# Moving the second weight's widening and part of the second inverse stage behind the first group

## The chip, the cores and the metric

The kernel runs on one core of one Trainium2 chip. The time is device microseconds of that core, the median of several executions. The engines are PE (matmuls), DVE (elementwise, two-input arithmetic), ACT (copies and activations), POOL (elementwise from on-chip memory) and SP, whose queue issues every DMA of this kernel. Each engine works its own instructions off in order.

## The reference

```python
# x: (8, 3136, 256); filt_r, filt_i: (1569, 256); w_ch1: (256, 1024); w_ch2: (1024, 256)
X = np.fft.rfft(x, axis=1)
y = np.fft.irfft(X * (filt_r + 1j * filt_i), n=3136, axis=1)
u = y + np.real(np.fft.fft(np.fft.fft(y, axis=1), axis=2))
un = (u - mean(u)) / np.sqrt(var(u) + 1e-6)        # over the last axis
out = u + np.maximum(un @ w_ch1, 0) @ w_ch2
```

## The kernel before, in words

Eight batches go through two pipelines that share the engines.

**The transform pipeline**, once a batch. `forward1` loads seven pieces of x (L379), takes their largest value (L267) to set a scale (`pow2` on DVE, PE and DVE again, then `spread`), splits x into a high and a low half (L394, L395), multiplies (L400) and stores the result in DRAM as d1 (L404). `forward2` loads d1 back as `at` (L425), multiplies with the second stage's table (L449, L450), applies the filters, and runs the first inverse stage (`inverse1`, L514 to L516), whose result goes to DRAM as d2 (L520). `inverse2` is the second inverse stage. It has 14 pieces c = 0 to 13: a load `b` for each pair of pieces (L554), four or eight matmuls (L577, called y_c below), a scaling copy on ACT into `ys` (L584), and, after each pair, four to six stores into DRAM as dy (L560). A pair covers 224 of the batch's 1568 slots.

**The group pipeline**. The slots of all batches are cut into groups of 256. `fetch(g)` reads a group's dy back (L633), `prepare(g)` adds the channel mix (L646 on PE, L656 on DVE), normalizes (L713 to L736) and makes two half-precision halves u16 (L739, L741). For group 0 the transposed `ut` comes from PE transposes (`flip`, L274 and L275); later groups use a DMA transpose (L746). Then eight steps f: `first_product` makes h (six matmuls L770, then L779 on ACT and L780 on DVE), and `second_product`, two steps later, adds twelve matmuls L799 into acc. The result goes through L808 to the output (L811). A group needs both weights: w1s in the first product, w2s in the second.

**The weights** come as 64-bit words. `widen_weights(i)` makes 32-bit numbers of piece i (0 to 3 are w1, 4 to 7 are w2) with four DVE instructions (L819, L820, L821, L825) and three on ACT (L824 between L820 and L825, and the two rows of L829, a sum of squares). `bound_weights` turns the sums into a scale (L865 to L868, with one PE transpose), `split_weights` spreads it with one PE matmul (called pb_w2 for w2; L263, L264), scales on ACT (L882), makes the high half on ACT (L883) and the low half on POOL (L884).

**What sets the order.** The program is written in an order of its own; a scheduler then orders each engine's queue, and `after(...)` puts the instructions of a block behind a marked instruction on its engine. `weigh(n)` emits the weight steps whose number in WIDEN_AT, BOUND_AT and SPLIT_AT is at most n; `give(n)` emits pieces of the second inverse stage, and `bring(slot)` as many as a slot needs. Before group 0 is fetched, pieces 0 to 3 of batch 0 are emitted. While `prepare(0)` runs, each of its steps is followed by another piece and by weight steps up to that number. The first steps of group 0 start at the lines after `bring(511)`.

Of the kernel before, what the change touches and what calls it, by code (L numbers as in the profile page):

```python
# [45 lines left out]
LOAD_AT = (19, 20, 21, 22, 50, 50, 54, 54)  # L46
LOAD_AFTER = (("d1", 10), ("d1", 11), ("d1", 12), ("d1", 13), ("bt", 3), ("bt", 3), ("bt", 4), ("bt", 4))
LOAD_IN = ("ut", "ut", "ys", "ys", "big", "big", "big", "big")
WIDEN_AT = (58, 59, 60, 61, 62, 63, 64, 65)
BOUND_AT = (62, 66)  # L50
SPLIT_AT = (63, 115)
FILTERS_AT = (2, 0, 1, 4, 6, 3, 8, 5)
FILTERS_ON_ACT = (0, 3, 4, 6)

# [140 lines left out]
def _program(ctx, tc, nc, a, NB):  # L195
# [6 lines left out]
    ps_f = ctx.enter_context(tc.tile_pool(name="ps_f", bufs=4, space=PSUM))  # L202
# [3 lines left out]
    marks = {}  # L206

    def bank(name):
        return ps_f.tile([128, 512], F32, tag="psf", name=name)
# [4 lines left out]
    def after(*keys):  # L214

        order = ExitStack()
        for k in keys:
            if k in marks:
                order.enter_context(tc.issue_after(marks[k]))
        return order  # L220
# [9 lines left out]
    ident16 = cp.tile([128, 128], F16, name="ident16")  # L230
# [38 lines left out]
    def flip(dst, src, pool, tag, name):  # L269

        m, n, q = src.shape
        pt = pool.tile([128, 8, 128], F16, tag=tag, name=name)
        for i in range(n):
            nc.tensor.transpose(pt[:q, i, :m], src[:, i], ident16[:m, :m])  # L274
        return nc.scalar.copy(dst, pt[:q, :n, :m])  # L275


# [360 lines left out]
    def channels(p, lhs, start, stop):  # L638

        work = [  # L640
# [3 lines left out]
        ]  # L644
        for i, (c0, n, hs, hm, w0) in enumerate(work):
            nc.tensor.matmul(  # L646
                p[:, c0 : c0 + n],
                lhs(int(i > 2), hs),
                mix[:, hm, w0 : w0 + n],
                start=start and i == 0,  # L650
                stop=stop and i == 7,
            )
# [5 lines left out]
    def add(o, pm, al):  # L658

        n = o.shape[0]  # L660
        oh = o.rearrange("p k (h c) -> p (k h) c", h=2)
        even = pm[:, 1:128].unsqueeze(1).to_broadcast([n, 4, 127])
        odd = pm[:, 129:].unsqueeze(1).to_broadcast([n, 2, 127])
        ends = pm[:, 0:129:128].unsqueeze(1).to_broadcast([n, 2, 2])
        scaled_add(oh[..., 1:], even, al[:, 0:1], oh[..., 1:])
        for hs, sign in ((slice(0, 4, 3), 0), (slice(1, 3), 1)):
            scaled_add(oh[:, hs, 1:], odd, al[:, sign : sign + 1], oh[:, hs, 1:])
        scaled_add(o[..., 0:129:128], ends, al[:, 0:1], o[..., 0:129:128])
# [9 lines left out]
    def prepare(g):  # L678
        tiles = groups[g]
        y = ys_of.pop(g)  # L680
        pm = bank(f"mix_{g}").rearrange("p (t c) -> p t c", t=2)
        fix = []
        for t, (g0, g1) in enumerate(tiles):
            n = g1 - g0
            r0 = g0 % RING
            channels(pm[:n, t], lambda e, h: eo[:, e, h, r0 : r0 + n], t == 0, t == len(tiles) - 1)
            for b in range(NB):
                if g0 <= b * NS < g1:
                    p0 = b * NS - g0
                    pn = bank(f"nyq_{g}_{t}")[p0 : p0 + 1, :256]  # L690
                    channels(pn, lambda e, h: esps[b][:, h, e : e + 1], True, True)
                    fix.append((t, slice(p0, p0 + 1), pn, alphas[b]))
            mixed[0] = g1
            yield
        for t, s, _, _ in fix:
            keep = mp.tile([128, 2, 256], F32, tag="un", name=f"keep_{g}", bufs=2)[:, 0]
            nc.scalar.copy(keep[s], y[s, t, 1])
        for t, (g0, g1) in enumerate(tiles):
            ps = slice(0, g1 - g0)
            with after(("u16", 0)) if g == 1 else after("h"):  # L700
                add(y[ps, t], pm[ps, t], alpha_of(g0, g1, f"al_{g}_{t}")[ps])
        for t, s, pn, al in fix:
            add_nyquist(y[s, t, 1], pn, al[s], keep[s])
        yield
        ut = mp.tile([128, 2, 8, 128], F16, tag="ut", name=f"ut_{g}", bufs=2)
        mv = tp.tile([128, 4, 2], F32, tag="mv", name=f"mv_{g}")
        st = tp.tile([128, 4, 6], F32, tag="st", name=f"st_{g}")
        n = tiles[0][1] - tiles[0][0]
        nt = 2 * len(tiles)
        for t, (g0, g1) in enumerate(tiles):  # L710
            m = g1 - g0
            for k in range(2):
                nc.vector.bn_stats(st[:m, 2 * t + k], y[:m, t, k])  # L713
                nc.vector.bn_aggr(mv[:m, 2 * t + k], st[:m, 2 * t + k])
        sb = tp.tile([128, 4, 4], F32, tag="sb", name=f"sb_{g}")
        parts = [(n, slice(0, nt))]
        if len(tiles) == 2 and tiles[1][1] - tiles[1][0] != n:
            parts = [(n, slice(0, 2)), (tiles[1][1] - tiles[1][0], slice(2, 4))]
        for m, ks in parts:
            nc.scalar.activation(sb[:m, ks, 0], mv[:m, ks, 1], AF.Sqrt, bias=eps[:m])  # L720
        yield
        for m, ks in parts:
            mu, v = mv[:m, ks, 0], mv[:m, ks, 1]
            r, q, c, s = (sb[:m, ks, i] for i in range(4))
            nc.vector.reciprocal(r, r)
            nc.vector.scalar_tensor_tensor(q, r, -8.0, r, op0=ALU.mult, op1=ALU.mult)
            nc.vector.scalar_tensor_tensor(c, v, EPS, q, op0=ALU.add, op1=ALU.mult)
            nc.vector.scalar_tensor_tensor(s, c, 24.0, r, op0=ALU.add, op1=ALU.mult)
            marks["un", g] = nc.vector.scalar_tensor_tensor(q, mu, -1.0, s, op0=ALU.mult, op1=ALU.mult).ins  # L729
        yield  # L730
        for t, (g0, g1) in enumerate(tiles):
            m = g1 - g0
            un = mp.tile([128, 2, 256], F32, tag="un", name=f"un_{g}_{t}", bufs=2)
            for k in range(2):
                i = 2 * t + k
                nc.scalar.activation(un[:m, k], y[:m, t, k], AF.Identity, bias=sb[:m, i, 1:2], scale=sb[:m, i, 3:4])  # L736
            u16 = mp.tile([128, 2, 2, 2, 128], F16, tag="u16", name=f"u16_{g}_{t}", bufs=2)
            unv = un[:m].rearrange("p k (d q) -> p k d q", q=128)
            nc.scalar.copy(u16[:m, :, :, 0], unv)  # L739
            low = nc.vector if g < 2 else nc.gpsimd  # L740
            marks["u16", g] = low.tensor_tensor(u16[:m, :, :, 1], unv, u16[:m, :, :, 0], op=ALU.subtract).ins  # L741
            if g == 0:
                ub = u16[:m].rearrange("p k d l q -> p (k d l) q")
                flip(ut[:, t, :, :m], ub, ps_f, "psf", f"utt_{t}")
            else:
                marks["sp"] = marks["ut", g] = nc.sync.dma_start_transpose(  # L746
                    ut[:, t, :, :m], u16[:m].rearrange("p k d l q -> p (k d l q)")
                ).ins
            yield
        ready[g] = (y, ut)  # L750
# [146 lines left out]
    done, come = [0], [0]  # L897

    def advance(n):

        while done[0] < min(n, NB * STEPS):
            b, s = divmod(done[0], STEPS)
            if s == 0 and come[0] < BACK * (b - 1) + 1:
                return
            if s in folds and b * NS + folds[s] - RING > mixed[0]:
                return
            next(forth)
            done[0] += 1

    def give(n):  # L910

        while come[0] < min(n, NB * BACK) and done[0] >= STEPS * (come[0] // BACK + 1) - 1:
            next(home)
            come[0] += 1
# [11 lines left out]
    def bring(slot):  # L926
        advance(STEPS * (slot // NS + 1) - 1)
        give(need(slot))
        assert come[0] >= need(slot)

    todo = [(n, load_weights, i) for i, n in enumerate(LOAD_AT)]
    todo += [(n, widen_weights, i) for i, n in enumerate(WIDEN_AT)]
    todo += [(n, f, w) for f, at in ((bound_weights, BOUND_AT), (split_weights, SPLIT_AT)) for n, w in zip(at, ("w1", "w2"))]
    todo.sort(key=lambda t: t[0])
# [29 lines left out]
    fetch(0)  # L964
    for i, _ in enumerate(prepare(0)):
        weigh(STEPS + come[0] + i)
        give(come[0] + 1)
    with after(("un", 0)):
        weigh(1000)
    bring(511)  # L970
    fetch(1)
    work = prepare(1)
    for _ in range(AHEAD):
        next(work, None)
    per = NS // 32
    for q in range(8 * ng + LAG):
        g, f = divmod(q, 8)
# [70 lines left out]
```

## Time and profile before

| | |
|---|---|
| median of three runs | 1537.51 us (1533.45 to 1542.68) |
| the profiled execution's own time | 1535.77 us |
| its span | 1534.0 us |
| granted clock of PE, mean | 0.955 |
| PE busy | 1398.7 us (91% of the span) |
| DVE, ACT, POOL busy | 1092.8, 771.3, 539.9 us |

A row of the timeline gives the start and the length in us, the engine, the line, the operation, what it writes and reads, the shapes and how many instructions are merged; in brackets the idle time before it and what ended that. A row of the windows gives each engine's busy time in a stretch, with the number of instructions, and then PE's granted clock, the DMA share and GB/s.

### The profile page before, as it was taken

The page shows a single profiled execution, that of the slowest core. Times are in us where ns is not written, and L with a number is a line of the kernel's source. Part 1 is how long each engine was busy: PE and PEld are TensorE (multiplying, and loading weights), DVE is VectorE, ACT ScalarE, POOL GpSimd, SP SyncE. Part 2 cuts the span into 40 slices and gives each one's busy share as a digit, 9 for nine tenths or more (in the row PEclk, how much of TensorE's full clock was granted, in tenths as well). Part 3 has the DMA queues.
Part 4 walks back from the last instruction along what each step waited for, and adds up shares of the span by engine and source line. Part 5 has one row for each costly group of instructions (what it writes and reads, how often), then busy time and mean ns, then how long its engine had stood idle before and what let it go on. Part 6 is the DMA issues. An engine that isn't in the chain of part 4 may idle for free.

```text
span 1534.0 us, 30300 instructions
## 1 busy us (share of the span) xinstructions
PE 1398.7 (91%) x11331; PEld 934.1 (61%) x11331; DVE 1092.8 (71%) x2388; ACT 771.3 (50%) x1426; POOL 539.9 (35%) x682
## 2 busy tenths in 40 slices
PE   5454899787999999999999999899999999999998
PEld 1432567454665677566765677566665667666666
DVE  5576878586967887687758877688767877565562
ACT  4466545354545464474544654374644655443341
POOL 3652049205810195006720284016620284110110
PEclk8675999998999999999999999999999999999999
DMA  8868478959985797859986796859876896644320
GB/s 263 218 205 219 101 163 176 219 157 206 203 216 146 175 227 174 208 152 214 192 192 161 192 231 159 211 146 220 183 189 158 195 237 144 166 107 110 95 55 29
DMA packets 429491, 268.98 MB, mean 175 GB/s; under 512 B 218624, under 2 KB 395824, under 8 KB 429344
## 3 DMA queue, kind: packets, MB, share of 16 engines
q1 hardware_dynamic: 429344, 267.05, 72.5%
q8 instruction: 89, 1.46, 0.4%
q14 instruction: 58, 0.48, 0.1%
HBM read 113.36 MB, written 102.76 MB: 141 GB/s over the span
## 4 chain that ended last, share of the span: by engine, by line
PE 67%; DMA 11%; DVE 7%; issue 3%; POOL 3%; ACT 2%; SPq 1%; DVEq 0%; POOLq 0%; ACTq 0%
PE h L770 26%; PE acc L799 26%; DMA x<-x 3%; PE s L400 3%; PE y L577 3%; DMA at<-d 2%; PE mix L646 2%; DVE y L656 2%; PE i L514 1%; DMA b<-d 1%; PE i L516 1%; PE i L515 1%; PE s L449 1%; DVE mx L267 1%; PE s L450 1%
## 5 line engine op out<-in xcount | busy, mean ns | idle before, releaser
L770 PE MATMUL h<-ut,w1s 128*128 128x512 f16 x2352 | 590.8, 385 | 24.6 <-DVE h L780 20.5
L799 PE MATMUL acc<-w2s,h 128*128 128x256 f16 x4704 | 599.9, 274 | 1.3 <-DVE h L780 1.3
L799 PEld LDWEIGHTS <-h 128*128 128x128 f16 x4704 | 456.4, 98 | 146.8 <-issue 13.6
L779 ACT ACTIVATE h<-h 128x512 f16<-128x512 f32 x392 | 233.1, 595 | 411.9 <-PE h L770 404.6
L780 DVE SCALAR_TENSOR_TENSOR h<-h,h 128x512 f16<-128x512 f32 x392 | 267.6, 683 | 200.3 <-ACT h L779 199.3
L741 POOL TENSOR_TENSOR u<-un,u 128x512 f16<-128x512 f32 x94 | 107.8, 1163 | 758.0 <-ACT u L739 745.6
L770 PEld LDWEIGHTS <-w1s 128*128 128x128 f16 x2352 | 223.8, 99 | 236.7 <-issue 48.1
L656 DVE SCALAR_TENSOR_TENSOR y<-mix,alpha,y 128x508 f32<-128x508 f32 (+1 forms) x368 | 156.0, 474 | 8.2 <-PE mix L646 6.9
L736 ACT ACTIVATE un<-y,sb 128x256 f32<-128x256 f32 x196 | 101.8, 589 | 44.0 <-DVE sb L729 38.8
L469 POOL TENSOR_TENSOR y<-yt,y 128x448 f16<-128x448 f32 x105 | 108.4, 1036 | 16.5 <-ACT y L468 16.2
L584 ACT ACTIVATE ys<-y,alpha 128x512 f32<-128x512 f32 x112 | 76.1, 686 | 71.4 <-PE y L577 71.0
L519 DVE TENSOR_TENSOR bt<-i,bt 112x512 f16<-112x512 f32 x112 | 75.7, 682 | 49.1 <-ACT bt L518 47.4
L267 DVE TENSOR_REDUCE mx<-x 112x1 f32<-112x1024 f32 x56 | 67.7, 1214 | 52.0 <-DMA x<-x 52.0
L463 POOL TENSOR_TENSOR yt<-yt,t 128x224 f32<-128x224 f32 x112 | 73.9, 660 | 81.9 <-DVE t L459 53.6
L455 DVE SCALAR_TENSOR_TENSOR yt<-s,pF,ft 128x448 f32<-128x448 f32 x112 | 75.3, 675 | 37.7 <-PE s L450 34.9
L449 PE MATMUL s<-s,at 112*128 112x56 f16 x896 | 62.7, 191 | 32.6 <-DMA at<-d 28.1
L400 PE MATMUL s<-x,s 112*112 112x512 f16 x294 | 87.3, 388 | 3.9 <-ACT x L394 1.9
L577 PE MATMUL y<-b,i 112*64 112x512 f16 (+1 forms) x480 | 74.1, 396 | 18.1 <-DMA b<-d 17.9
L518 ACT CAST bt<-i 112x512 f16<-112x512 f32 x112 | 64.9, 585 | 49.9 <-PE i L516 43.7
L808 DVE SCALAR_TENSOR_TENSOR y<-acc,beta,y 128x512 f32<-128x512 f32 x98 | 71.2, 742 | 25.7 <-PE acc L799 25.5
L468 ACT CAST y<-yt 128x448 f16<-128x448 f32 x112 | 62.6, 564 | 38.6 <-POOL yt L464 35.6
L449 PEld LDWEIGHTS <-at 112*128 112x128 f16 x896 | 55.8, 98 | 42.6 <-DMA at<-d 36.0
(133 smaller groups left out, 1663.4 us busy)
## 6 DMA issues: line engine op xcount, KB each, us to landing
x<-x SPq DMA_DIRECT2D x56, 448.0 KB
d<-ast SPq DMA_DIRECT2D x112, 224.0 KB
at<-d SPq DMA_DIRECT2D x56, 448.0 KB
d<-bt SPq DMA_DIRECT2D x112, 224.0 KB
b<-d SPq DMA_DIRECT2D x56, 448.0 KB
out<-y SPq DMA_DIRECT2D x98, 256.0 KB
y<-dy SPq DMA_DIRECT2D x92, 256.0 KB
dy<-ys SPq DMA_DIRECT2D x208, 112.0 KB
```

The source lines that it names most:

```text
L267: nc.vector.tensor_reduce(dst, src, axis=axis, op=ALU.max, apply_absolute_value=True)
L400: nc.tensor.matmul(p, s1[:, hs], x16[:, hx], start=i == 0, stop=i == 2)
L449: nc.tensor.matmul(o, w, s2[:, U, 0].rearrange("p (r k) -> p r k", r=2), start=True, stop=False)
L469: last = half(b, hf == 1).tensor_tensor(ylo, ytv, yhi, op=ALU.subtract)
L577: nc.tensor.matmul(p[64 * h : 64 * h + 64, js], i2[:, t, h, i], bt[:, o + js.start : o + js.stop, h], start=i == 0, stop=i == 1,)
L656: nc.vector.scalar_tensor_tensor(out, p, al, y, op0=ALU.mult, op1=ALU.add)
L736: nc.scalar.activation(un[:m, k], y[:m, t, k], AF.Identity, bias=sb[:m, i, 1:2], scale=sb[:m, i, 3:4])
L741: marks["u16", g] = low.tensor_tensor(u16[:m, :, :, 1], unv, u16[:m, :, :, 0], op=ALU.subtract).ins
L770: marks["pe"] = nc.tensor.matmul(p[:, c0 : c0 + n].rearrange("p (t k q) -> p t k q", k=2, q=m), w1s[:, d, hw, 128 * f : 128 * f + 128], ut ...
L779: nc.scalar.activation(h[:, 0, :nt], p[:, :nt], AF.Relu)
L780: marks["h"] = nc.vector.scalar_tensor_tensor(h[:, 1, :nt], p[:, :nt], 0.0, h[:, 0, :nt], op0=ALU.max, op1=ALU.subtract).ins
L799: nc.tensor.matmul(acc[:m, k], h[:, hh, c0 : c0 + m], w2s[:, f, hw], start=f == 0 and k == 0 and i == 0, stop=f == 7 and k == 1 and i == 2,)
```

## The change

Two things move, and nothing is added or removed. The widening of pieces 5, 6 and 7, the bound and the split of w2 get numbers of 200 and more, so that `weigh` emits them only at `weigh(1000)`, behind the DVE instruction that ends group 0's normalization factors (marked "un"). And `prepare(0)` no longer gives a piece of the second inverse stage after each step: piece 4 and all later ones are emitted in `bring(511)` and afterwards, behind group 0's fetch on SP, its last transpose on PE and its last `ut` copy on ACT.

```diff
-WIDEN_AT = (58, 59, 60, 61, 62, 63, 64, 65)
-BOUND_AT = (62, 66)
-SPLIT_AT = (63, 115)
+WIDEN_AT = (58, 59, 60, 61, 62, 200, 200, 200)
+BOUND_AT = (62, 201)
+SPLIT_AT = (63, 202)
...
-            nc.tensor.transpose(pt[:q, i, :m], src[:, i], ident16[:m, :m])
+            marks["flip"] = nc.tensor.transpose(pt[:q, i, :m], src[:, i], ident16[:m, :m]).ins
...
-                flip(ut[:, t, :, :m], ub, ps_f, "psf", f"utt_{t}")
+                marks["ut0"] = flip(ut[:, t, :, :m], ub, ps_f, "psf", f"utt_{t}").ins
...
     for i, _ in enumerate(prepare(0)):
         weigh(STEPS + come[0] + i)
-        give(come[0] + 1)
     with after(("un", 0)):
         weigh(1000)
-    bring(511)
+    with after(("y", 0), "flip", "ut0"):
+        bring(511)
```

SP's queue around group 0's fetch, before (y_0 and y_1 are the groups' fetches, dy_0 the stores of batch 0, b2_0_k its loads for pieces 2k and 2k+1, x_1 the next batch's input):

```order
L560 DMA dy_0_1127<-ys_0_2_1184 28x4x256 x4
L554 DMA b2_0_3_1222<-d2_0_117 112x8x256
L560 DMA dy_0_1127<-ys_0_4_1224 28x4x256 x4
L554 DMA b2_0_4_1263<-d2_0_117 112x8x256
L560 DMA dy_0_1127<-ys_0_6_1265 28x4x256 x2
L633 DMA y_0_1201<-dy_0_1127 128x2x256 x2
L554 DMA b2_0_5_1300<-d2_0_117 112x8x256
L633 DMA y_1_1377<-dy_0_1127 128x2x256 x2
L379 DMA x_1_0_1449<-x 112x1024
```

The same place now:

```order
L560 DMA dy_0_1119<-ys_0_2_1149 28x4x256 x4
L633 DMA y_0_1166<-dy_0_1119 128x2x256 x2
L554 DMA b2_0_3_1311<-d2_0_117 112x8x256
L633 DMA y_1_1330<-dy_0_1119 128x2x256
L560 DMA dy_0_1119<-ys_0_4_1313 28x4x256 x4
L554 DMA b2_0_4_1400<-d2_0_117 112x8x256
L560 DMA dy_0_1119<-ys_0_6_1402 28x4x256 x2
L633 DMA y_1_1330<-dy_0_1119 128x2x256
L379 DMA x_1_0_1411<-x 112x1024
```

Group 0's fetch moves ahead of the loads b2_0_3 and b2_0_4 and of the six stores of pieces 4 to 7 that stood before it; the second half of group 1's fetch, which stood next to the first, now stands behind the stores of pieces 4 and 5.

PE's queue where w2's scale is spread, before (i2 is the second inverse stage's table, u16_0_0 a half of group 0):

```order
L577 MATMUL y_0_8_1303<-b2_0_4_1263,i2_85 64x512
L250 MATMUL pt_w2_1149<-ident_87,mw2_1076 1x128
L263 MATMUL pb_w2_1361<-row_w2_1151,ones_89 128x2
L274 LDWEIGHTS u16_0_0_1312
L274 MATMUL utt_0_1315<-ident16_88,u16_0_0_1312 128x128
```

The same matmul now, with h_0_0 the first product of group 0's first step:

```order
L250 MATMUL pt_w2_1286<-ident_87,mw2_1076 1x128
L577 LDWEIGHTS i2_85
L577 MATMUL y_0_8_1447<-b2_0_4_1400,i2_85 64x512
...
L577 MATMUL y_0_9_1489<-b2_0_4_1400,i2_85 64x512
L646 LDWEIGHTS eo_91
L646 MATMUL mix_2_1466<-mix_86,eo_91 128x129
...
L646 MATMUL mix_2_1466<-mix_86,eo_91 128x64
L263 MATMUL pb_w2_1295<-row_w2_1288,ones_89 128x2
L770 LDWEIGHTS w1s_94
L770 MATMUL h_0_0_1383<-ut_0_1209,w1s_94 128x512
```

The matmul pb_w2, which stood ahead of group 0's transposes, now stands behind them and behind pieces 4 to 9 (y_0_8 and y_0_9 need the load b2_0_4), directly ahead of group 0's first product. On DVE the copy that takes it out of PSUM (L264) stands behind all of group 1's additions (L656), which need the second half of group 1's fetch. The queues come together again: PE's is the same as before from row 4793 of 22578 on, DVE's from row 556 of 2111, ACT's from row 364 of 1315, POOL's from row 218 of 634 and SP's from row 257 of 860, all in the middle of batch 2.

## The prediction

> **What bounds the kernel now.** First the windows, cut where the chain changes hands:
>
> ```profile
> 108.00:126.80 18.80, 6.52 (x33) 2.40 (x32) 13.72 (x26) 14.06 (x30) 4.48 (x4) 0.59 0.87 233
> 126.80:147.40 20.60, 8.28 (x63) 5.58 (x63) 11.11 (x41) 11.81 (x22) 5.66 (x5) 0.52 0.79 190
> 147.40:175.40 28.00, 23.70 (x157) 15.23 (x156) 26.83 (x70) 13.01 (x25) 0.00 (x0) 0.97 0.40 105
> 175.40:282.00 106.60, 100.33 (x867) 68.39 (x868) 85.67 (x171) 59.18 (x113) 60.74 (x79) 0.96 0.74 166
> ...
> 358.70:1534.00 1175.30, 1146.02 (x9353) 769.98 (x9353) 837.68 (x1848) 587.44 (x1088) 406.45 (x509) 0.99 0.73 171
> ```
>
> After 358.7 us PE is busy for 1146.0 of 1175.3 us, so a shift there is carried to the end. The queues are in the old order from the middle of batch 2 on, so the change can act only ahead of that. The two windows up to 147.4 hold 24.6 us without PE work (39.4 less 6.52 and 8.28): there the change wants to gain. The timeline shows what they wait for:
>
> ```profile
> 108.11 2.02 SPq L560 DMA_DIRECT2D dy<-ys  x4
> 114.55 1.65 SPq L560 DMA_DIRECT2D dy<-ys  x4
> 116.30 0.34 SPq L554 DMA_DIRECT2D b<-d  x1
> 118.69 0.91 SPq L633 DMA_DIRECT2D y<-dy  x2
> 120.98 1.06 PE L577 MATMUL y<-b,i 112*64 112x512 f16 x4 [3.56 <-DMA b<-d]
> 123.76 0.40 ACT L697 COPY keep<-y 1x256 f32<-1x256 f32 x1
> 126.80 2.43 DVE L656 SCALAR_TENSOR_TENSOR y<-mix,alpha,y 128x508 f32<-128x508 f32 x5
> 134.99 2.07 ACT L736 ACTIVATE un<-y,sb 128x256 f32<-128x256 f32 x4 [1.05 <-DVE sb L729]
> 136.97 2.54 ACT L882 ACTIVATE w<-w,sw 128x512 f32<-128x512 f32 x4
> 140.05 1.29 DVE L741 TENSOR_TENSOR u<-un,u 128x512 f16<-128x512 f32 x2 [4.83 <-ACT u L739]
> 143.68 1.90 ACT L275 COPY ut<-utt 128x1024 f16<-128x1024 f16 x2
> 147.45 2.76 PE L770 MATMUL h<-ut,w1s 128*128 128x512 f16 x12
> 150.05 0.60 PE L799 MATMUL acc<-w2s,h 128*128 128x256 f16 x4
> ```
>
> Group 0's fetch is issued at 118.69, 8.56 us after the stores that it reads (108.11 + 2.02 = 110.13), because SP works off other stores and loads first. The first addition waits until 126.80 though the fetch has landed by 123.76: DVE widens until then. First product at 147.45, first acc at 150.05.
>
> **Part 1, the early fetch.** On SP it now stands directly behind its stores. How long it waits for them the trace shows only for a neighbour, in the chain of waits:
>
> ```profile
> 117.85 2.60 DMA dy<-ys
> ```
>
> Two stores, 2.60 us from first issue to landing. I take 113.0 for the fetch (110.13 + 2.6, rounded up) and, from issue to first addition, 3.8 us; the bounds are 2.6 (this row) and 5.07 (118.69 to the copy at 123.76, a copy that had ACT work ahead of it). First addition at 116.8, between 115.6 and 118.1, against 126.80: 10.0 us earlier. [...]
>
> **Part 2, group 0 up to its last half.** From the first addition to the normalization (126.80 to 134.99) is 8.2 us. One widening instruction leaves this stretch, which I count at nothing to be careful; but w1's scaling on ACT, which ran earlier, now lands in it: four L882 as at 136.97, 2.54, less what hides behind the statistics: I count 1.8. So the normalization starts at 116.8 + 10.0 = 126.8. From there to the last u16 (134.99 to 141.34, 6.35 us) the four L882 of w2 leave ACT (2.54), and piece 5 comes in. It costs by these rows:
>
> ```profile
> L819 DVE TENSOR_SCALAR cv<-raw x8: 404/420/1378, 95.9 to 122.4; 128x512 int32<-128x512 int32 x8
> L820 DVE SCALAR_TENSOR_TENSOR w<-raw,cv x8: 673/692/1526, 96.6 to 123.8; 128x512 int32<-128x512 int32 x8
> L824 ACT ACTIVATE cv<-raw x8: 647/660/675, 97.3 to 125.3; 128x512 f32<-128x512 f32 x8
> L829 ACT ACTIVATE wsq<-w x8: 620/630/631, 99.5 to 129.9; 128x512 bf16<-128x512 f32 x8
> L884 POOL TENSOR_TENSOR w1s<-w,w1s x4: 1152/1464/1596, 122.3 to 126.3; 128x512 f16<-128x512 f32 x4
> ```
>
> A piece takes DVE 2.5 us by the medians (0.42 + 3 x 0.69), but 1.38 and 1.53 an instruction beside POOL's L884; piece 5 now meets the four L884 of w1 (5.6 us), so I take 5.1. Net 6.3: the last u16 is ready at 133.1 (141.34 before, 8.2 us earlier).
>
> **Part 3, the scale of w2.** Here the lead is spent. Pieces 6 and 7 follow on DVE and ACT (their cost beside other work is in the next sum); pieces 4 and 5 of the inverse stage run on PE behind the transposes. The rows for this sum:
>
> ```profile
> 133.64 0.30 ACT L720 ACTIVATE sb<-mv,eps 128x4 f32<-128x4 f32 x1 [1.26 <-DVE row_w L253]
> 140.45 2.17 ACT L883 CAST w2s<-w 128x512 f16<-128x512 f32 x4
> 145.69 1.28 PE L646 MATMUL mix<-mix,eo 128*128 128x129 f16 x14
> L584 ACT ACTIVATE ys<-y,alpha 128x512 f32<-128x512 f32 x112 | 76.1, 686 | 71.4 <-PE y L577 71.0
> L779 ACT ACTIVATE h<-h 128x512 f16<-128x512 f32 x392 | 233.1, 595 | 411.9 <-PE h L770 404.6
> 166.82 0.69 DVE L780 SCALAR_TENSOR_TENSOR h<-h,h 128x512 f16<-128x512 f32 x1
> ```
>
> ACT then has the two `ut` copies (1.90), one L824 and one L829 (0.66 + 0.63) and two scaling copies (2 x 0.69), 4.6 us, behind the transposes of the last u16: `ys` of piece 5 is ready at 138. Its stores take 1.65 (as at 114.55), the load b2_0_4 is issued at 140, and from issue to matmul a load took 4.68 (116.30 to 120.98): piece 8 runs at 144.7. With piece 9 (1.06 each) and thirteen mix matmuls (1.28 for fourteen) that is 3.3 us of PE, of which some lies ahead of the load; pb_w2 at 147.6. The other leg: group 1's second fetch waits for the same stores (140 + 2.6 less what the issue took, 142), stands behind that load and lands in 3.8 to 5.1, at 146.4; four additions and two statistics (2.4, as at 126.80) end at 148.8. Both legs meet in L264: scale at 149. Then L882 2.54, L720 0.30, three L883 1.63, L779 0.60, L780 0.69: first acc at 154.8, against 150.05. That is 4.8 us later, in spite of a fetch that was 10 us earlier; between 151 and 159 by the bounds of the three DMA steps (1.2 each way) and DVE's two prices. The 24 us hole stays, its wait has another name.
>
> **Part 4, group 0's eight steps.**
>
> ```profile
> 153.47 2.33 DVE L267 TENSOR_REDUCE mx<-x 112x1 f32<-112x1024 f32 x2
> 175.39 5.28 PE L770 MATMUL h<-ut,w1s 128*128 128x512 f16 x12 [0.83 <-DMA ut<-u]
> 273.28 4.24 PE L770 MATMUL h<-ut,w1s 128*128 128x512 f16 x12 [3.25 <-DMA ut<-u]
> 238.84 1.31 PE acc L799 x12
> 316.47 1.29 PE h L770 x6
> ```
>
> Between the first acc and the seventh L780 DVE now has seven L780 (4.6), seven L267 (8.2), two L741 of group 1 (1.3), group 2's additions (2.2), and waits 1.6 for ACT, which makes group 1's `un` between the second and third step: 17.9, to 172.7, and group 1 starts at 174.0. Before it started at 175.39, because its `ut` landed late; now `ut` is transposed ten us ahead. But at that point PE still owes 20 acc matmuls, 7 of L400 and 4 of L577 that it had done before: 20 x 0.109 (12 in 1.31) + 11 x 0.215 (6 in 1.29) = 4.5 us. Against that, the twelve products at 175.39 took 5.28 after the stall instead of 2.76 as at 147.45; without it 2.5 us are saved. Net: 4.5 - 1.4 - 2.5 = +0.6 us. [...]
>
> **Part 5, batches 1 and 2.** From 175.4 to 282 PE is busy for 100.33 of 106.6 us, so progress is PE work. The last product of batch 1's first inverse stage has 6 L770 and 11 L799 more ahead of it than before: 2.5 us. Its store releases what follows:
>
> ```profile
> 282.33 3.84 DMA d<-bt
> 289.56 12.27 DMA b<-d
> 353.40 5.30 DMA at<-d
> PE s L449 <- DMA at<-d: 11.4, 2, 10.4
> ```
>
> Through b, x and `at` of batch 2 the chain reaches 358.7, where PE has waited 10.4 us: a delay at 282 appears there in full, and PE has then done the same work in both. Sum: +0.6 + 2.5 = **+3.1 us**. The profiled execution's own time, 1535.77, becomes 1538.9; the median of the runs shown is 1.74 above it, so I forecast **1540.6**, 0.2% slower.
>
> **The rivals.** A measurement of this kernel can tell about 0.5%, 7.7 us, from no change.
>
> *Slower: batch 1's start is what counts.* Its first product (L400) now has 30 more L770 and 28 more L799 ahead of it, and starts 11.7 us after group 1 (30 x 0.215 + 48 x 0.109), at 185.7 instead of 172.2. If the way from there to 282 is bound by its own loads and by POOL, not by PE's work, the 13.5 us stay: 1535.8 + 13.5 + 1.7 = 1551. It decides if more than some 6 us of PE's work between cannot be moved into its waits. For it: POOL is busy for 60.74 us there. Against: PE idles only 6.3 us of 106.6. Chance 0.20.
>
> *Faster: the lead survives.* If the two loads land as DVE comes to them (143), the fetch takes 2.6 and POOL doesn't slow piece 5, the first acc comes at 148.3 and the sum is -3.4. With that, the 24 L799 and 7 L770 that batch 2's scale no longer has behind it must shorten its forward stage by their 4.1 us, so that the wait of 10.4 shrinks: -7.5, 1530. All of it at once, or more: 0.14.
>
> *No change.* Only some of that comes together, or the wait of 10.4 us takes in what was lost: -3 to 0, 1534 to 1537.5. For it: three of the terms are DMA latencies that I rounded up. Chance 0.25.
>
> *The forecast,* +0 to +7: 0.41.
>
> **How the numbers follow.** The range reaches from the low end of the third case with most of the second to just above the slow rival: 1529 to 1552; under and above lie about 0.1 each. Faster by over 0.5%: 0.14. Slower by over 0.5%: 0.20. Within: 0.66, the third case and the forecast.
>
> **What would show it.** Right: the fetch on SP near 113, first addition near 117, the normalization near 127, pb_w2 directly ahead of the first product with an idle PE before it, first acc near 155, no wait for `ut` at group 1 and no low clock there, batch 1's first L400 near 186, batch 2's L449 some 3 us later than 358.7. Wrong: the first acc at or before 150, or batch 2's `at` more than 8 us away from its old place.

## The result and the profile after

The changed kernel takes 1552.3 us in the median of four runs (1550.65 to 1556.18), against 1535.74 us (1533.45 to 1542.68) of the kernel before in four: a ratio of 1.0112, 95% interval 1.008 to 1.0145. It is slower by about 1%, where 1540.6 was forecast and 1552 was the upper end of the range. Of the rivals, the one called "batch 1's start is what counts" gave 1551.

First the timeline of the changed kernel, at the steps that the prediction had dated:

```profile
110.76 3.68 SPq L633 DMA_DIRECT2D y<-dy  x2
115.19 0.75 DVE L656 SCALAR_TENSOR_TENSOR y<-mix,alpha,y 128x508 f32<-128x508 f32 x1 [2.11 <-ACT keep L697]
128.34 2.08 ACT L736 ACTIVATE un<-y,sb 128x256 f32<-128x256 f32 x4 [2.88 <-DVE sb L729]
143.94 1.06 PE L577 MATMUL y<-b,i 112*64 112x512 f16 x4 [2.68 <-DMA b<-d]
146.50 1.78 DVE L656 SCALAR_TENSOR_TENSOR y<-mix,alpha,y 128x508 f32<-128x508 f32 x4 [4.21 <-DMA y<-dy]
147.34 0.58 PE L263 MATMUL pb_w<-row_w,ones 1*128 1x2 f32 x2
154.07 0.61 PE L799 MATMUL acc<-w2s,h 128*128 128x256 f16 x4
171.29 0.15 DVE L385 TENSOR_REDUCE mx<-mx 112x1 f32<-112x7 f32 x1
172.56 1.46 PE L770 MATMUL h<-ut,w1s 128*128 128x512 f16 x6
184.69 0.38 PE L400 MATMUL s<-x,s 112*112 112x512 f16 x1
372.36 0.23 PE L449 MATMUL s<-s,at 112*128 112x56 f16 x1 [6.50 <-DMA at<-d]
377.80 1.46 PE L770 MATMUL h<-ut,w1s 128*128 128x512 f16 x3 [0.55 <-DMA ut<-u]
```

The first seven rows are the chain of group 0, and it went as forecast within 2.3 us: fetch 110.8 (113 forecast), first addition 115.2 (117), normalization 128.3 (127), piece 8 at 143.9 (144.7), group 1's second half at 146.5 (146.4), pb_w2 at 147.3 (147.6), first acc at 154.1 (154.8). Group 1 starts at 172.6 without a wait (174.0), batch 1's first L400 at 184.7 (185.7). The last two rows are batch 2's first L449 and the first product of group 6, the first group that needs batch 1's result. The same points of the kernel before:

```profile
164.45 0.15 DVE L385 TENSOR_REDUCE mx<-mx 112x1 f32<-112x7 f32 x1
172.23 0.38 PE L400 MATMUL s<-x,s 112*112 112x512 f16 x1 [1.71 <-ACT x L394]
358.75 0.23 PE L449 MATMUL s<-s,at 112*128 112x56 f16 x1 [10.37 <-DMA at<-d]
361.77 1.46 PE L770 MATMUL h<-ut,w1s 128*128 128x512 f16 x3
```

L400 is 12.5 us later, batch 2's L449 13.6, group 6 16.0. None of the 12.5 us is made up in the stretch between L400 and batch 2's L449. That stretch by the windows, of the kernel before and then of the changed one:

```profile
172.20:358.70 186.50, 160.18 (x1247) 103.52 (x1246) 139.48 (x284) 95.29 (x177) 63.01 (x81) 0.93 0.74 177
```

```profile
184.70:372.40 187.70, 155.03 (x1195) 101.11 (x1194) 131.94 (x274) 90.76 (x166) 61.14 (x80) 0.91 0.71 171
```

It holds 5.2 us less PE work than before and lasts 1.2 us longer. And the groups of instructions, from the start of the span to batch 2's first L449, again before and then after:

```profile
L770 PE MATMUL h<-ut,w1s 128*128 128x512 f16 x288 | 76.3, 400 | 8.0 <-DMA ut<-u 4.1 <-DVE h L780 3.9
L799 PE MATMUL acc<-w2s,h 128*128 128x256 f16 x576 | 73.9, 274 | 1.3 <-DVE h L780 1.3
```

```profile
L799 PE MATMUL acc<-w2s,h 128*128 128x256 f16 x576 | 78.3, 281 | 4.4 <-DVE y L808 4.4
L770 PE MATMUL h<-ut,w1s 128*128 128x512 f16 x288 | 75.4, 397 | 5.5 <-DVE h L780 4.1 <-DMA ut<-u 1.4
```

Both have done 288 L770 and 576 L799 by then: all six groups that batch 0 can feed. There is no more group work until batch 1 delivers group 6. What PE does ahead of L400 is not gained, it is missing behind it.

### The profile page after: what moved, and what is told of

Read it like the earlier page. It is cut to its first block, busy times and chain, and to the rows that moved or that the text cites. A ratio compares the mean times of both kernels' runs of the same rounds, so it can differ in the third digit from the quotient of the medians.

```text
span 1551.5 us, 30301 instructions
## 1 busy us (share of the span) xinstructions
PE 1408.6 (91%) x11331; PEld 941.9 (61%) x11331; DVE 1093.8 (71%) x2388; ACT 771.5 (50%) x1426; POOL 540.0 (35%) x682
## 4 chain that ended last, share of the span: by engine, by line
PE 62%; DMA 10%; issue 8%; DVE 6%; POOL 4%; ACT 3%; SPq 1%; DVEq 0%; POOLq 0%; ACTq 0%
PE h L770 25%; PE acc L799 24%; DMA x<-x 3%; PE s L400 3%; PE y L577 3%; DMA at<-d 2%; DMA y<-dy 2%; PE mix L646 2%; DVE y L656 2%; PE i L514 1%; PE i L516 1%; PE i L515 1%; PE s L449 1%; DMA d<-ast 1%; DVE h L780 1%
## 5 line engine op out<-in xcount | busy, mean ns | idle before, releaser
L770 PE MATMUL h<-ut,w1s 128*128 128x512 f16 x2352 | 590.7, 385 | 23.0 <-DVE h L780 21.0
L799 PE MATMUL acc<-w2s,h 128*128 128x256 f16 x4704 | 602.8, 274 | 6.0 <-DVE y L808 6.0
L799 PEld LDWEIGHTS <-h 128*128 128x128 f16 x4704 | 457.2, 98 | 152.5 <-issue 18.6
L741 POOL TENSOR_TENSOR u<-un,u 128x512 f16<-128x512 f32 x94 | 108.5, 1170 | 754.7 <-ACT u L739 742.3
L770 PEld LDWEIGHTS <-w1s 128*128 128x128 f16 x2352 | 224.1, 99 | 234.9 <-issue 45.7
L656 DVE SCALAR_TENSOR_TENSOR y<-mix,alpha,y 128x508 f32<-128x508 f32 (+1 forms) x368 | 156.2, 474 | 10.3 <-DMA y<-dy 4.8
L449 PE MATMUL s<-s,at 112*128 112x56 f16 x896 | 65.1, 194 | 33.4 <-DMA at<-d 28.2
L400 PE MATMUL s<-x,s 112*112 112x512 f16 x294 | 88.7, 391 | 3.5 <-DVE x L395 1.6
L577 PE MATMUL y<-b,i 112*64 112x512 f16 (+1 forms) x480 | 73.7, 396 | 14.9 <-DMA b<-d 14.5
L449 PEld LDWEIGHTS <-at 112*128 112x128 f16 x896 | 58.1, 100 | 43.5 <-DMA at<-d 36.6
```

The costliest lines, as they stand in the source:

```text
L400: nc.tensor.matmul(p, s1[:, hs], x16[:, hx], start=i == 0, stop=i == 2)
L449: nc.tensor.matmul(o, w, s2[:, U, 0].rearrange("p (r k) -> p r k", r=2), start=True, stop=False)
L577: nc.tensor.matmul(p[64 * h : 64 * h + 64, js], i2[:, t, h, i], bt[:, o + js.start : o + js.stop, h], start=i == 0, stop=i == 1,)
L656: nc.vector.scalar_tensor_tensor(out, p, al, y, op0=ALU.mult, op1=ALU.add)
L770: marks["pe"] = nc.tensor.matmul(p[:, c0 : c0 + n].rearrange("p (t k q) -> p t k q", k=2, q=m), w1s[:, d, hw, 128 * f : 128 * f + 128], ut ...
L799: nc.tensor.matmul(acc[:m, k], h[:, hh, c0 : c0 + m], w2s[:, f, hw], start=f == 0 and k == 0 and i == 0, stop=f == 7 and k == 1 and i == 2,)
```

## The experiments

Theory A: batch 1's way through its DRAM stages takes as long whatever PE does beside it, so its late start is what costs. Theory B: what costs is w2's late scale and the late first acc. Theory C, the step of the prediction: between 175 and 282 us progress is PE's work. All kernels below come to the old queue order again in batch 2, and each ratio is against the kernel before on the same chip.

**Delay batch 1 in the kernel before.**

```diff
-            with after(("y", 1), ("un", 0)) if b == 1 else nullcontext():
+            with after(("b", 6)) if b == 1 else nullcontext():
```

> The kernel before, with nothing of the change; only batch 1's seven input loads are held behind the load b2_0_6 on SP instead of behind group 1's fetch. Group 0, group 1's start and w2's scale keep their places; batch 1's first L400 moves behind 18 more L770 and 16 more L799 (5.6 us of PE work), its first L449 behind 18 more L770 and 45 more L799 (18 x 0.215 + 45 x 0.109 = 8.8 us), and PE's queue is the old one again from row 4793 on. Theory A (batch 1's chain through its two DRAM stages takes as long whatever PE does beside it, so a later start reaches the end in full): first acc unchanged near 150, batch 1's L449 8 to 11 us later, and 9 to 14 us slower than before. Theory B (what costs is w2's late scale and the late first acc of group 0): no change, within 3 us. Theory C (the step of the prediction: from there on progress is PE's work, and work moved ahead of the chain is not done behind it): 0 to 3 us slower.

Measured: 1551.06 us, ratio 1.0101 (1.0081 to 1.012). Its timeline:

```profile
152.23 0.60 PE L799 MATMUL acc<-w2s,h 128*128 128x256 f16 x4
189.18 0.38 PE L400 MATMUL s<-x,s 112*112 112x512 f16 x1
370.57 0.23 PE L449 MATMUL s<-s,at 112*128 112x56 f16 x1 [7.02 <-DMA at<-d]
378.97 1.25 PE L770 MATMUL h<-ut,w1s 128*128 128x512 f16 x5 [1.56 <-DMA ut<-u]
```

The first acc is 2.2 us late, L400 17.0 and group 6 17.2. With nothing of the change in it, this kernel loses as much as the change does. B and C fall here. A had 9 to 14 us for the time; the medians are 15.3 apart. The queue's count (5.6 us of PE work) was too small for L400, since batch 1's largest values (L385) come 9.3 us late as well.

**The two parts alone.** The first takes only the three tables of the change, the second only its other lines.

> The first part of the change alone: the second weight's widening, bound and split are held behind group 0's normalization, the pieces of the second inverse stage stand as before. Batch 1's first L449 has 18 more L770 and 43 more L799 ahead of it than before (8.6 us of PE work). Theory A: 8 to 15 us slower than before, in step with batch 1's first L449. Theory B: by how much the first acc comes later than 150; the pieces stay ahead of it, so I expect 155 or later and 5 to 15 us slower. Theory C: 0 to 5 us slower.

Measured: 1532.98 us, ratio 0.9989 (0.9972 to 1.0006), no difference. First acc at 150.8, L400 at 177.5, group 6 at 360.7. A had 8 to 15 us and was wrong: L400 had 48 more matmuls ahead of it, but group 1 started at 167.1, 8.3 us early, so they were done sooner. And the 5.3 us by which L400 is late all the same are made up behind it: group 6 is 1.1 us early.

> The second part of the change alone: pieces of the second inverse stage are held behind group 0, the second weight is widened and split as before. w2's scale is spread ahead of the pieces 6 to 9 (20 L577 ahead of it against 44 in the changed kernel), but batch 1's first L400 has 36 more L770 and 40 more L799 ahead of it than before (12.1 us), its first L449 24 and 61 (11.8 us): later in the queue than in the changed kernel. Theory A: 12 to 19 us slower than before, though the first acc comes early. Theory B: the first acc at or before 150, so 0 to 8 us faster than before. Theory C: within 3 us of before.

Measured: 1550.36 us, ratio 1.0083 (1.0057 to 1.0109). The first acc comes at 145.1, 4.9 us early, and the kernel is slower all the same: B falls again. L400 is at 187.3, group 6 at 378.5. The loss comes with the held pieces, not with the weights.

**Start batch 1's steps earlier in the changed kernel.**

```diff
-RISE = 28
+RISE = 20
```

> The changed kernel with RISE 20 instead of 28, so that batch 1's transform steps are written earlier between the groups' steps (batches 2 to 7 keep their pace). Group 0 and w2's scale stay as in the changed kernel. Against before, batch 1's first L400 has 18 more L770 and 6 more L799 ahead of it (changed kernel: 30 and 28), its first L449 6 more L770 and 19 more L799 (changed kernel: 18 and 52): 3.4 us instead of 9.5. Theory A: L449 of batch 1 some 6 us earlier than in the changed kernel, and the end with it: 5 to 9 us faster than the changed kernel, 6 to 12 slower than before. Theory B: first acc stays near 154, so no gain over the changed kernel: 15 to 18 slower than before. Theory C: within 3 us of the changed kernel as well.

Measured: 1551.07 us, ratio 1.009 (1.0069 to 1.0112): nothing gained over the changed kernel that the intervals could tell. Batch 1's first L449 came at 215.4, only 2.2 us later than before, so the theory that this point alone decides is wrong. But group 6 starts at 372.6, 10.8 us late: its transposed `ut` is what PE waits for (6.3 us). Batch 1's chain has two ends, `at` of batch 2 and the `ut` of group 6, and the one that comes last counts.

**Put group 1 behind batch 1 again**, so that PE's queue in the changed kernel is the old one from L400 on.

```diff
-                nc.tensor.matmul(p, s1[:, hs], x16[:, hx], start=i == 0, stop=i == 2)
+                marks["s1", b, q] = nc.tensor.matmul(p, s1[:, hs], x16[:, hx], start=i == 0, stop=i == 2).ins
...
-            first_product(g, f)
+            with after(("s1", 1, 2)) if q == 8 else nullcontext():
+                first_product(g, f)
```

> The changed kernel with one order more: group 1's first product is held behind batch 1's third step on PE, so that from there on PE's queue stands as before the change (48 L770 and 96 L799 ahead of the first L400 instead of 78 and 124; 114 and 192 ahead of the first L449, as before). Group 0 and w2's scale stay as in the changed kernel. Theory A (batch 1's chain through its DRAM stages sets the time at which group 6 can start, and group work done ahead of it is not missed by PE but not used either): group 1 starts later than in the changed kernel, 178 to 182, batch 1's first L449 comes back to 214 to 218, group 6 to within 2 to 6 us of its old start, 9 to 14 us faster than the changed kernel and 2 to 6 slower than before. Theory B (w2's late scale and first acc, or the work that PE owes for it): first acc stays near 154 and group 1 starts later still, so as slow as the changed kernel or slower, 15 to 22 above before.

Measured: 1545.74 us, ratio 1.007 (1.0042 to 1.0097). The timeline:

```profile
177.22 0.38 PE L400 MATMUL s<-x,s 112*112 112x512 f16 x1 [1.00 <-ACT x L394]
363.16 0.23 PE L449 MATMUL s<-s,at 112*128 112x56 f16 x1 [7.05 <-DMA at<-d]
371.15 1.46 PE L770 MATMUL h<-ut,w1s 128*128 128x512 f16 x3 [0.74 <-DMA ut<-u]
```

Group 1 (181.5) and batch 1's first L449 (216.6) came as A had said, and the first acc stayed where it was (153.7). But group 6 is still 9.4 us late, 5 more than batch 2's L449, and the time is 9.7 us above before by the medians, where A had 2 to 6: only some 40% of the loss is gone.

**Let batch 1's input in early in the changed kernel.**

```diff
-            with after(("y", 1), ("un", 0)) if b == 1 else nullcontext():
+            with after(("y", 0)) if b == 1 else nullcontext():
```

> The changed kernel with batch 1's seven input loads held only behind group 0's fetch on SP, not behind the whole of group 1's: the first stands five places earlier. PE's order stays as in the changed kernel up to row 1107 and DVE's up to row 403, batch 1's first L400 still behind 78 L770 and 124 L799. If the queue's order sets batch 1's start (theory A, as I hold it): the input lands 10 to 20 us earlier and L400 still comes at 182 to 185, within 3 us of the changed kernel's time, 14 to 18 above before. If the late input sets it (theory A with another cause): L400 at 175 to 179, 5 to 10 us faster than the changed kernel.

Measured: 1546.17 us, ratio 1.007 (1.0042 to 1.0098). L400 at 185.1: as expected, the early input doesn't move it, since DVE's largest values stand where they stood (L385 at 171.4). The kernel is some 6 us faster than the changed one nevertheless. Batch 2's first L400 comes at 330.5 instead of 338.5 and group 6 at 371.9; by the queue it has 6 L770 and 23 L799 fewer ahead of it. A had at most 3 us for the gain; the other theory had 5 to 10, but by way of an earlier L400, which didn't come. No expectation had this way.

**Both at once.**

> Both at once: the changed kernel with group 1's first product held behind batch 1's third step on PE, and with the input loads held only behind group 0's fetch. Theory A: the input is early and the place in PE's queue is the old one, so L400 is limited by DVE's largest values alone and comes at or before 174; L449 at or before 214, group 6 within 2 us of its old start or earlier: 13 to 18 us faster than the changed kernel, within 4 us of before. Theory B: as slow as the changed kernel, 13 to 20 above before. If only the input's lateness mattered: the same gain as with the early input alone.

Measured: 1534.6 us, ratio 0.9996 (0.9977 to 1.0015): the whole loss is gone.

```profile
176.62 0.38 PE L400 MATMUL s<-x,s 112*112 112x512 f16 x1 [1.00 <-ACT x L394]
358.39 0.94 PE L770 MATMUL h<-ut,w1s 128*128 128x512 f16 x2
```

The change's group 0 and its late w2 (first acc at 152.1) cost nothing measurable once group 6 is back in its place. B is out. But L400 is still 4.4 us later than before, behind A's 174, while group 6 is 3.4 us earlier: a late L400 doesn't reach the end in full here either.

**Leave PE work out of the kernel before.**

```diff
-                for hw, hx in ((0, 0), (0, 1), (1, 0)):
+                for hw, hx in ((0, 0), (0, 1), (1, 0))[: 2 if g in (3, 4, 5) else 3]:
...
-                        stop=i == 5,
+                        stop=i == (3 if g in (3, 4, 5) else 5),
```

> The kernel before, with work left out: groups 3, 4 and 5 leave out the third of the three products of each half (w1's high half with the low half of the input), 2 of 6 L770 in each of their 24 steps, 48 matmuls or 48 x 0.215 = 10.3 us of PE's work. All of it lies between batch 1's first L400 and batch 2's first L449. Queue orders are the old ones up to PE's row 2349 and again from row 4793 on (less the rows left out). Theory A (the chain of batch 1 and batch 2 through DRAM sets the time there and the groups' products only fill its waits): batch 2's L449 0 to 3 us earlier, 0 to 3 us faster than before. Theory C (the step of the prediction: progress there is PE's work): batch 2's L449 8 to 10 us earlier, 8 to 10 us faster.

(The product left out is w1's low half with the input's high half; the expectation names the halves the wrong way round.) Measured: 1534.35 us, ratio 1.001 (0.9992 to 1.0029). The stretch from L400 to batch 2's L449 by the windows, and group 6's start by the timeline:

```profile
173.80:354.90 181.10, 153.32 (x1199) 100.83 (x1198) 140.20 (x281) 96.22 (x177) 62.98 (x81) 0.91 0.75 182
```

```profile
365.59 1.46 PE L770 MATMUL h<-ut,w1s 128*128 128x512 f16 x3 [3.33 <-DMA ut<-u]
```

10.3 us of PE's work are gone and the time is the same, where C had 8 to 10 us. Batch 2's L449 is 3.8 us earlier, outside what A had said and less than half of what C had; group 6 is 3.8 us later. C is out in its size. That nothing at all was gained is not shown, since SP's order changed with the work left out (below). Of the 10.3 us only 6.9 show as less busy time in the stretch (160.18 less 153.32), at a granted clock of 0.91 where it was 0.93 (taken to full clock, an estimate, the two are 139.5 and 149.0 us, 9.5 apart).

**Four on the way to a faster kernel:** the same order in the kernel before; in the weights' part alone; in the weights' part with the early input; and in the weights' part with `q == 7` for `q == 8`, which holds group 0's last step as well.

> The kernel before with group 1's first product held behind batch 1's third step on PE and nothing else: its first L400 keeps 48 L770 and 96 L799 ahead of it, its first L449 has 6 L770 and 6 L799 fewer (1.9 us). It tells how much of the gain of the weights' part with this order (5.6 us) is the order's alone. Theory A: L449 0 to 2 us earlier, 0 to 3 us faster than before; the rest of the gain is then group 0's earlier steps. If the order alone brings the gain: 5 to 6 us faster.

Measured: 1528.91 us, ratio 0.9958 (0.9943 to 0.9974): the order alone brings the gain, 6.0 us by the medians, where A had at most 3. Group 6 at 356.4.

> The weights' part of the change alone, with the same order more (group 1's first product behind batch 1's third step on PE). With the weights' part alone batch 1's first L400 came at 177.5 and its first L449 at 215.4, 5.3 and 2.2 us later than before, and group 6 at 360.7, 1.1 us earlier than before; it had 24 L770 and 24 L799 more ahead of L400, which now stand behind it. Theory A: L400 near 172, L449 2 to 5 us earlier than with the weights' part alone, group 6 with it: 3 to 8 us faster than before. Theory B: group 1 starts later than at 167, the gain of the weights' part is lost: 0 to 5 us slower than before.

Measured: 1530.46 us, ratio 0.9967 (0.9948 to 0.9986). L400 at 172.6, group 6 at 358.4, as A had said; but by the run above this owes little to the weights' part.

> The weights' part with that order, and batch 1's input loads held only behind group 0's fetch (as in the run with both on the whole change, where it brought 11 us over the order alone). With the weights' part and the order alone the loads were issued at 135.8 to 139.4 and L400 came at 172.6. Theory A: the largest values and L400 come up to 3 us earlier, 0 to 4 us faster than that kernel, 5 to 10 faster than before. If the early loads delay group 0's and group 1's fetches on SP: first acc later than 151.4 and no gain.

Measured: 1537.66 us, ratio 1.0028 (1.001 to 1.0045), though the first acc came at 149.9 and L400 at 172.0. Group 6 starts at 361.3, as in the kernel before: the early loads, which gained 11 us in the changed kernel with the order, cost 7 here by the medians (9 by the ratios). A had a gain of 0 to 4. Why isn't shown.

> The weights' part with group 0's last step held behind batch 1's third step as well (not group 1's first): 42 L770 and 84 L799 ahead of the first L400 instead of 48 and 96, 102 and 176 ahead of the first L449 instead of 114 and 192 (4.3 us). Theory A: if L400 can come earlier, up to 4 us faster than with group 1 held; but the largest values end at 166 and the scale needs some 6 us more, so L400 stays at 171 to 173, PE waits, and the time is within 2 us of that kernel (3 to 8 us faster than before). Theory B: group 0's end is late, 0 to 5 us slower than before.

Measured: 1526.22 us, ratio 0.995 (0.993 to 0.997): the lowest median of all, below both kernels, though its interval overlaps with that of the order in the kernel before. L400 is at 174.1, 1.8 us late, and the first acc at 154.3, 4.3 us late, but group 6 at 354.7, 7.1 us early. A had 3 to 8 us; the medians are 8.7 apart.

**All runs side by side**, by the start of group 6 (the timeline's first L770 behind batch 2's first L449; the shift is against 361.8 of before):

| kernel | batch 1's L400 | group 6 | shift | ratio |
|---|---|---|---|---|
| batch 1 delayed | 189.2 | 379.0 | +17.2 | 1.0101 |
| pieces' part | 187.3 | 378.5 | +16.8 | 1.0083 |
| the change | 184.7 | 377.8 | +16.0 | 1.0112 |
| RISE 20 | 180.3 | 372.6 | +10.8 | 1.009 |
| early input | 185.1 | 371.9 | +10.2 | 1.007 |
| order | 177.2 | 371.2 | +9.4 | 1.007 |
| work left out | 173.8 | 365.6 | +3.8 | 1.001 |
| weights, order, early input | 172.0 | 361.3 | -0.5 | 1.0028 |
| weights' part | 177.5 | 360.7 | -1.1 | 0.9989 |
| order, early input | 176.6 | 358.4 | -3.4 | 0.9996 |
| weights, order | 172.6 | 358.4 | -3.3 | 0.9967 |
| before, order | 173.9 | 356.4 | -5.4 | 0.9958 |
| weights, order from q = 7 | 174.1 | 354.7 | -7.1 | 0.995 |

Group 6's start ranks all thirteen nearly as the measured times do; L400 does so only roughly, and the first acc not at all. The dates come from one execution of each kernel: L400 came 1.6 us later than before in two kernels (work left out; before, order) that have the same 48 L770 and 96 L799 ahead of it, so a shift of that size says nothing.

Theory A doesn't hold as it was put. From L400 to group 6 the thirteen kernels take between 180.6 and 193.9 us (189.5 before), so the way itself varies as much as the delay of L400 in the changed kernel, and A's times were missed in at least seven of the twelve runs. What holds is that group 6's start carries the loss. What sets the length of the way is open. An untested rival is DVE's queue: in the profile's chain of the kernel before, from batch 2's first L400 (320.15) to its load of `at` (353.40), some 18 of 33 us are instructions on DVE (L403, L395, L656 above all), and no run takes work off DVE.

**Where group 6 falls behind batch 2's L449**, SP's queue shows it. In five of the fourteen traces (before; early input; order, early input; weights, order; before, order) group 6 starts 3.0 to 3.2 us behind batch 2's first L449, and there the first transpose of its `ut` (L746) is issued ahead of `at` (L425). In the other nine it starts 5.2 to 10.7 us behind, and the transpose is issued behind two or three loads of `at`, mostly behind stores, a load b or a fetch as well. The kernel before, then the one with work left out:

```profile
351.92 1.26 SPq L746 DMA_TRANSPOSE ut<-u  x1
353.40 1.05 SPq L425 DMA_DIRECT2D at<-d  x2
354.50 3.50 SPq L746 DMA_TRANSPOSE ut<-u  x1
```

```profile
350.19 1.50 SPq L425 DMA_DIRECT2D at<-d  x3
351.79 2.08 SPq L554 DMA_DIRECT2D b<-d  x1
353.98 2.51 SPq L633 DMA_DIRECT2D y<-dy  x2
356.54 5.64 SPq L746 DMA_TRANSPOSE ut<-u  x2
```

The halves u to be transposed (L741 on POOL) were done at 353.0 in the first and at 353.3 in the second, although 10.3 us of PE's work are gone there: up to that point PE's work had not been the limit. The 3 us after that are the place in SP's queue; by batch 2's L449, with 3.0 us behind it, group 6 could have come at 357.9, so some 4 us at most (an estimate) may be hidden by that place. No run moves this transpose alone.

## Why the prediction was wrong

- **Parts 1 to 3** were right: every date within 2.3 us, the early fetch, the lead spent on w2's scale, the first acc 4.0 us later (4.8 forecast). In part 2 errors cancelled. Its second sum doesn't follow from its terms: 6.35 less 2.54 with 5.1 for piece 5 is 8.9 us and not 6.3, which comes out with the price of 2.5. The trace has 4.9 us (128.34 to 133.22), because piece 5 came after POOL's L884 and cost 2.5. L884 ran beside the normalization factors instead, where four small instructions took 4 us (below), so the stretch before took 13 us and not 10.
- **Part 4** was right in kind: no wait for `ut` at group 1, which starts 2.8 us earlier than before (1.4 forecast). Nor was there a low clock: the granted one was 1.00 from 172.56 to 184.70, where before it was 0.50 over the 5.28 us from 175.39.
- **Part 5 failed**, at "From 175.4 to 282 PE is busy for 100.33 of 106.6 us, so progress is PE work". It put +2.5 us where the trace shows +14.0 at batch 1's last store and +16.0 at group 6. A PE that is 94% busy was taken for the bound. By batch 2's L449 both kernels have done the same limited stock of group work; with 10.3 us of it left out, L449 came only 3.8 us earlier and the time was the same. The 30 L770 and 28 L799 that moved ahead of L400 left longer waits behind it (PE without work for 32.7 us of the stretch instead of 26.3) and no shorter chain.
- **The wait of 10.4 us** for batch 2's `at` was quoted as the place where a delay appears in full. That reading fits: batch 2's L449 is 13.6 us late. And it spoke against part 5: a wait on a DMA at the end of the stretch says that the chain came last there, and not PE's work.
- **The slow rival** had the mechanism, the 13.5 us (12.5 measured at L400) and the time, 1551. Its point of decision, whether PE's work between would fit into the waits, isn't what the runs follow: the stretch lasts 186.5 us with 160 us of work, 187.7 with 155 and 181.1 with 153. That its sum came within 1.3 us of the measured time is in part luck: the 12.5 us at L400 grew to 16.0 at group 6 and 17.5 at the end, and in two other runs a late L400 (5.3 and 4.4 us) cost nothing. Its chance of 0.20 was too low, and the range ended 0.3 us below the measured time.
- **The change's aim** was met in its first half: group 0's normalization begins 6.7 us earlier. The loss came from the pieces held back, with which the queue puts batch 1's scale and first products later; the held weights alone cost nothing.

What stays open: between group 9 (+14.9 us) and the end (+17.5) the profiled execution loses 2.6 us more in single steps, as other runs do by up to 7 us (RISE 20) with the same queue order, and no run separates these steps. Open too is what sets the time from L400 to group 6, which differs by 13 us between the kernels.

## What to carry to other kernels

A busy engine is not the bound if its work is a fixed stock that fills another chain's waits: look for the wait at the end of the stretch, and count whether the same work is done at that point in both orders. When a change moves work ahead of the start of a chain through DRAM, put the chain's whole delay among the likely outcomes; here it reached the end in the changed kernel and with batch 1 delayed, but not in two runs with a delay of 4 to 5 us. To settle it, leave filling work out, and look at all queues first: a scheduler lays them anew, and here the order on SP changed with it.

## What the runs showed of the hardware

Four small DVE instructions took 0.81 to 1.08 us each while POOL ran L884, and 0.16 or 0.17 us with POOL idle. In the changed kernel, POOL's row and then DVE's, at w1's low half; the last four rows are the same four instructions for group 2 with POOL idle:

```profile
123.79 4.49 POOL L884 TENSOR_TENSOR w1s<-w,w1s 128x512 f16<-128x512 f32 x4 [19.23 <-ACT w1s L883]
124.17 0.81 DVE L726 SCALAR_TENSOR_TENSOR sb<-sb 128x4 f32<-128x4 f32 x1
125.01 1.08 DVE L727 SCALAR_TENSOR_TENSOR sb<-mv,sb 128x4 f32<-128x4 f32 x1
126.12 1.08 DVE L728 SCALAR_TENSOR_TENSOR sb<-sb 128x4 f32<-128x4 f32 x1
127.23 1.08 DVE L729 SCALAR_TENSOR_TENSOR sb<-mv,sb 128x4 f32<-128x4 f32 x1
...
176.55 0.17 DVE L726 SCALAR_TENSOR_TENSOR sb<-sb 128x4 f32<-128x4 f32 x1
176.75 0.17 DVE L727 SCALAR_TENSOR_TENSOR sb<-mv,sb 128x4 f32<-128x4 f32 x1
176.95 0.17 DVE L728 SCALAR_TENSOR_TENSOR sb<-sb 128x4 f32<-128x4 f32 x1
177.77 0.16 DVE L729 SCALAR_TENSOR_TENSOR sb<-mv,sb 128x4 f32<-128x4 f32 x1
```

Together the four took 4.05 us, 3.4 us more than the 0.67 with POOL idle. The last three started 1.11 us apart, about one L884 (4.49 / 4 = 1.12). That they waited for it is an inference from these rows; no run takes L884 away.

And the granted clock differed between the kernels. The last 35.2 us up to batch 2's L449 in the windows, of the kernel before and of the one with 48 matmuls fewer:

```profile
323.50:358.70 35.20, 22.74 (x153) 13.26 (x151) 29.97 (x74) 19.75 (x36) 2.27 (x2) 0.85 0.67 186
```

```profile
319.70:354.90 35.20, 24.07 (x128) 11.62 (x127) 29.98 (x70) 21.05 (x38) 2.26 (x2) 0.77 0.64 184
```

With 25 matmuls fewer in it the granted clock is 0.77 instead of 0.85. Over the stretch from L400 to batch 2's L449 it was 0.91 in the changed kernel (1195 matmuls) and with work left out (1199), 0.92 with batch 1 delayed (1216), 0.93 before (1247), 0.94 with the order and the early input (1251) and with the order (1252), and 0.96 with the order in the kernel before (1247). But the number alone doesn't rank every stretch: from 323.5 to 358.7 the kernel with work left out had 169 matmuls at 0.71, the kernel before 153 at 0.85. What sets the clock no run separates.
